# Two transformer layers on one Trainium2 core: the opening's order list, and norm sums of three head groups moved behind the first transposes and widened to 80 columns

## The chip, the cores and the metric

The kernel runs on one core of one Trainium2 chip. The time is device time of the whole program in microseconds (us); lower is better. Inside the core, TensorE (PE) multiplies matrices into the eight PSUM banks, ScalarE (ACT) does exponentials and other functions, VectorE (DVE) and GpSimd (POOL) do elementwise work, and SyncE (SP) issues the DMAs.

## What is computed

Two layers, each an attention block and a mixer block, over 2048 tokens of 448 features in bf16:

```python
def _A_ref(x, wqkv, wo):              # 16 heads of 28 features
    qkv = (x @ wqkv).reshape(B, S, 3, H, Dh) ...
    scores = einsum("bhqd,bhkd->bhqk", q, k) * (Dh ** -0.5)
    p = softmax(scores); o = einsum("bhqk,bhkd->bhqd", p, v)
    return o.reshape(B, S, D) @ wo

x = x + _A_ref(layernorm(x), A_wqkv, A_wo)
x = x + _B_ref(layernorm(x), B_w1, B_w2, B_w3, B_w4)   # token-shift mixer and a gelu MLP
...                                                    # and both once more, same weights
```

All inputs are drawn at random; x and the weights of the attention have a scale of 0.05.

## The kernel before

The 16 heads lie in four groups of four; a group's four heads take the four 32-row strips of TensorE. Tokens lie in 16 tiles of 128. Scores are computed transposed (keys on partitions), exponentiated by ScalarE in pieces of two or three PSUM banks (L1822, `PT`), or for some pieces by VectorE and GpSimd (L1703 to L1720), and multiplied with V (L1855). Instead of a row maximum the softmax uses a bound: it adds to Q's 29th row a shift made of the largest squared norm of K (`kmaxc`), and takes off a multiple of Q's own squared norm. The multiples come from the norms of the weight columns of Q and K.

Those norms are what the change touches. `wnorm(s)` in `t_setup` makes them, with s = 0 for head group 0 and s = 1 for groups 1 to 3. It squares the weights of K and Q (L1275 on ScalarE or L1277 on VectorE), adds each column over 448 rows with matmuls against a column of ones (L1282: 8 matmuls for s = 0, 24 for s = 1), copies the sums to `csum` (L1286), adds them per head with the 0/1 matrix `a28` (L1287), copies to `wsum` (L1289), and with a few small operations (L1291 to L1302, a power on GpSimd at L1296) makes `ACOL` and `RTN`. Q's update (L1511) needs the first, the bias (L1613) the second.

The opening, before the first exponential, holds: the loads of x and of the K, Q and V weights; layer-norm statistics of the first four tiles (L1345 to L1447), their normalized copies `xn` (L1449 or L1451), the transposes on TensorE (`pe_transpose`, L1403) and their copies to `xT` (L1409 or L1411); K and Q projections of the four groups (`kq_proj`: four column strips of 32 in each of four 512-column matmuls, L1458), whose PSUM results are evicted with a scale (L1463, L1465, L1470), squared (L1474 or L1478) and summed per head (L1195); V projections (L1195) and their evictions (L1531).

The order of work isn't that of the source. A planner runs all generators twice against a table of costs (`dur`, `lat`, `svc`) and makes a list of operations for each engine. `OTHER` then names operations that go to their second engine (`alt`: an eviction to ScalarE in place of VectorE, for instance, or the other way round), and `ENGINE_ORDER` permutes each engine's list; in its text the numbers are, in turn, how many entries to take and how far to jump. `follow` walks the permuted lists, assigns PSUM banks, derives the semaphore waits, and calls `keep_pe_busy`: where its costs leave a gap on TensorE that is long enough, and TensorE's use over the last 4 us of its reckoning is not above 80%, it puts in 256-column matmuls of ones into a free bank (filler, L2246), whose result nobody reads. `GATE1` to `GATE3` name events that some generators wait for in the planner.

Each engine runs its list strictly in order. In the plan of dependencies, `reads` and `writes` are keys such as `("wst", 1)` for K's weights; a key in `reads` makes an operation wait for whoever writes it.

Of the kernel before, what the change touches and what calls it, by code (L numbers as in the profile page):

```python
# [756 lines left out]
def build_kernel(nc, A_x, A_wqkv, A_wo, B_x, B_w1, B_w2, B_w3, B_w4, out, n_layers=2):  # L757
    S = A_x.shape[1]
    D = 448
# [343 lines left out]
    def c_act(n):  # L1103
        return 0.08 + n * 0.000833
# [1238 lines left out]
```

## Time and profile before

| | |
|---|---|
| median of 3 runs | 1023.48 us (1022.03 to 1023.53) |
| profiled execution | 1021.86 us, span 1020.1 us |
| mean granted TensorE clock | 0.998 |
| busy in the span | ACT 985.9, PE 960.7, DVE 830.3, POOL 164.0 us |

A span is the time from the first to the last instruction on record. A row of a group gives line, engine, operation, output and input by the program's names, the number of instructions, busy time, the mean duration in ns, and the idle time ahead of them with what ended it. A row of the timeline gives the start, the time to the end of the last of the merged instructions, and then the same names; instructions that run one into the other are merged, and matmul ends are modelled.

### The profile page before, as it was taken

How to read it: one execution, taken by the hardware profiler on the slowest of the kernel's cores; microseconds unless marked ns; L12 is line 12 of the kernel's file. 1: busy time of each engine (PE TensorE's matmuls, PEld its weight loads, DVE VectorE, ACT ScalarE, POOL GpSimd, SP SyncE). 2: the span in 40 equal slices, each digit the busy share in tenths (PEclk: the TensorE clock that was granted, in tenths of full speed). 3: DMA queues.
4: the chain of work that ended last, by engine and by line, in shares of the span. 5: the costliest groups of instructions: out<-in, count | busy, mean ns of one | idle time of the engine just before them, and what ended most of it. 6: DMA issues, size and time to landing. Idle time of an engine off the chain costs nothing.

```text
span 1020.1 us, 24089 instructions
## 1 busy us (share of the span) xinstructions
PE 960.7 (94%) x10399; PEld 362.4 (36%) x10414; DVE 830.3 (81%) x1868; ACT 985.9 (97%) x941; POOL 164.0 (16%) x187
## 2 busy tenths in 40 slices
PE   9989899999999999999999999988999999999998
PEld 5322222333232333332343443332233233444456
DVE  8987887788978779888788888788888878878663
ACT  6999999999999999999999999999999999999983
POOL 3000101201110112112122020012222020121211
PEclk9999999999999999999999999999999999999999
DMA  5245311010101002210111101411020000110000
GB/s 140 55 102 148 87 37 22 3 36 1 22 1 22 2 1 43 38 22 1 22 43 32 28 22 43 115 43 42 22 38 8 14 20 6 22 31 2 11 11 23
DMA packets 70722, 35.21 MB, mean 35 GB/s; under 512 B 56472, under 2 KB 65048, under 8 KB 70616
## 3 DMA queue, kind: packets, MB, share of 16 engines
q1 hardware_dynamic: 70616, 33.68, 14.3%
q8 instruction: 81, 1.33, 0.5%
q14 instruction: 25, 0.20, 0.1%
HBM read 12.70 MB, written 7.08 MB: 19 GB/s over the span
## 4 chain that ended last, share of the span: by engine, by line
ACT 83%; PE 13%; DMA 1%; DVE 1%; SPq 0%; issue 0%; DVEq 0%
ACT PT L1822 76%; PE ps L1192 4%; ACT h2T L2211 4%; PE ps L1794 3%; PE ps L1195 3%; PE ps L1855 2%; ACT gt L1992 1%; PE ps L1458 1%; ACT L2211 1%; DMA uin<-uscr 1%; DMA wk_raw<-in_A_wqkv_dram 1%; ACT L1822 0%; DMA uscr<-uin 0%; DVE uin L1900 0%; SPq L1397 0%
## 5 line engine op out<-in xcount | busy, mean ns | idle before, releaser
L1822 ACT ACTIVATE PT<-ps 128x1024 bf16<-128x1024 f32 (+1 forms) x821 | 886.4, 1252 | 5.4 <-PE ps L1794 3.7
L1794 PE MATMUL ps<-qT,kT 32*128 32x512 bf16 x1536 | 247.3, 384 | 38.8 <-ACT PT L1822 28.9
L1855 PE MATMUL ps<-PT,vaug 128*32 128x512 bf16 (+1 forms) x2181 | 268.1, 361 | 2.5 <-ACT PT L1822 0.8
L1794 PEld LDWEIGHTS ps<-qT,kT 32*128 32x128 bf16 x1536 | 61.4, 91 | 243.8 <-ACT PT L1822 190.5
L1716 POOL TENSOR_TENSOR gt<-gt 128x512 f16<-128x512 f16 x55 | 59.8, 1088 | 473.8 <-DVE gt L1714 470.7
L1855 PEld LDWEIGHTS ps<-PT,vaug 128*32 128x32 bf16 x2181 | 76.8, 94 | 106.5 <-issue 76.4
L1192 PE MATMUL ps<-xT,w 112*128 112x512 bf16 (+6 forms) x514 | 105.9, 320 | 0.1
L1703 DVE TENSOR_SCALAR t<-ps 128x512 int32<-128x512 f32 x112 | 76.6, 684 | 25.1 <-PE ps L1794 23.7
L2171 DVE CAST h2T<-ps 128x512 bf16<-128x512 f32 (+2 forms) x126 | 72.3, 581 | 26.3 <-PE ps L1192 13.2
L1794 PE MATMUL ps<-kT 32*128 32x256 bf16 (+1 forms) x768 | 82.8, 310 | 8.0 <-ACT PT L1822 5.4
L1720 DVE SCALAR_TENSOR_TENSOR PTD<-t,gt 128x512 uint16<-128x512 int32 x112 | 78.2, 701 | 5.4 <-PE ps L1855 1.9
L1195 PE MATMUL ps<-xT,w 112*32 112x512 bf16 (+3 forms) x1048 | 81.9, 344 | 0.6 <-DVE h2T L2171 0.6
L1717 DVE SCALAR_TENSOR_TENSOR gt<-gt,t 128x512 f16<-128x512 f16 x112 | 77.7, 695 | 4.7 <-POOL gt L1716 3.7
L2246 PE MATMUL ps<-ones_bf 128*128 128x256 bf16 x334 | 60.6, 282 | 1.8 <-DVE wk_raw L1246 1.2
L1195 PE MATMUL ps<-w,h2T 128*32 128x448 bf16 x932 | 57.7, 353 | 1.8 <-ACT h2T L2211 1.5
L1192 PEld LDWEIGHTS ps<-xT,w 112*128 112x128 bf16 (+1 forms) x514 | 40.9, 103 | 43.0 <-issue 23.4
L1192 PE MATMUL ps<-w,h2T 128*128 128x448 bf16 x215 | 52.1, 355 | 0.0
L1714 DVE TENSOR_SCALAR gt<-t 128x512 f16<-128x512 uint16 x112 | 48.5, 436 | 1.6
L1794 PEld LDWEIGHTS ps<-kT 32*128 32x128 bf16 x768 | 23.2, 91 | 74.8 <-ACT PT L1822 54.7
L2211 ACT ACTIVATE h2T<-h2T 128x7168 bf16<-128x7168 bf16 (+2 forms) x9 | 44.9, 5012 | 0.1
L1458 PE MATMUL ps<-xT,wq_raw 112*32 112x512 bf16 (+1 forms) x576 | 44.7, 363 | 0.3 <-issue 0.3
L1458 PE MATMUL ps<-xT,wk_raw 112*32 112x512 bf16 (+3 forms) x640 | 42.9, 348 | 0.4 <-DVE hT L1959 0.4
(157 smaller groups left out, 1148.6 us busy)
## 6 DMA issues: line engine op xcount, KB each, us to landing
uin<-uscr SPq DMA_DIRECT2D x20, 256.0 KB, 2.7
uscr<-u_sb SPq DMA_DIRECT2D x12, 256.0 KB, 2.1
uscr<-uin SPq DMA_DIRECT2D x8, 256.0 KB, 2.2
out_dram<-uin SPq DMA_DIRECT2D x16, 112.0 KB, 1.7
w<-in_B_w_dram SPq DMA_DIRECT2D x4, 392.0 KB, 5.1
x_res<-in_A_x_dram SPq DMA_DIRECT2D x3, 448.0 KB, 8.7
w<-in_B_w_dram SPq DMA_DIRECT2D x2, 448.0 KB, 4.0
w<-in_B_w_dram SPq DMA_DIRECT2D x4, 196.0 KB, 4.0
```

Source lines behind the costliest of these rows:

```text
L1192: return e.matmul(out=dst(0, m), lhsT=lhs(0, m), rhs=rhs() if callable(rhs) else rhs, start=start, stop=stop)
L1195: return [e.matmul(out=dst(a, min(m, a + 32)), lhsT=lhs(a, min(m, a + 32)), rhs=rhs() if callable(rhs) else rhs, start=start, stop=stop, t ...
L1458: yield op("pe", c_mm(nw) + Sched.COLT, lambda e, b=b, fc=fc, rows=rows: [e.matmul(out=ps[32 * j:32 * j + 32, bi(b), 0:nw], lhsT=w[0:rows, ...
L1703: yield op("dve", c_ps(512), lambda e: e.tensor_scalar(out=t32[:, ti.n, :], in0=ps[:, bk, :], scalar1=0.0, scalar2=65536.0, op0=ALU.max, o ...
L1717: yield op("dve", c_ps(512), lambda e: e.scalar_tensor_tensor(out=half(), in0=half(), scalar=EXPV * 2.0 ** -16, in1=frac(), op0=ALU.add, o ...
L1720: yield op("dve", c_ps(512), lambda e: e.scalar_tensor_tensor(out=PTD[:, to.n, :].bitcast(mybir.dt.uint16), in0=t32[:, ti.n, :], scalar=2. ...
L1794: yield op("pe", 0.005 if ph == h else 0.012 + W / 2400.0, lambda e, bk=bk, r0=32 * j, g=g, kc=kc, qt=qt, q0=q0, W=W, c0=W * h: e.matmul(o ...
L1822: yield op("act", e_dur(n), lambda e, b0=b0, p0=p0, cnt=cnt: e.activation(out=PT[:, p0:p0 + cnt, :], in_=ps[:, b0:b0 + cnt, :], func=ACT.E ...
L1855: return e.matmul(out=ps[32 * j:32 * j + 32, UBK, 0:128 * nt], lhsT=vaug[:, vs, 32 * (4 * g + j):32 * (4 * g + j) + 32], rhs=rhs(), start= ...
L2171: yield op("dve", c_ps(NW), lambda e, fch=fch, b=b: e.tensor_copy(out=h2T[:, fch, hoff:hoff + NW], in_=ps[:, bi(b), 0:NW]), reads=[("ps", ...
L2211: yield op("act", c_act(14 * NW), lambda e, c0=c0, NW=NW: e.activation(out=h2T[:, :, c0:c0 + NW], in_=h2T[:, :, c0:c0 + NW], func=ACT.Gelu ...
L2246: SC.fill = (0.13, lambda e, b: e.matmul(out=ps[:, bi(b), 0:256], lhsT=ones_bf[:, :], rhs=ones_bf[:, :].unsqueeze(1).to_broadcast([128, 2, ...
```

## The change

Four things are edited. First, the 24 sums of `wnorm(1)` also read `("lnT", k)` for k = 0 to 3, a new key that the copy of a transposed tile (L1409 or L1411) writes; for `wnorm(0)` that list is empty. `GATE3`, which was empty, makes the planner start `wnorm(1)` after the event `("ln", 0, 0)`, when the first four tiles have been transposed. Second, every sum of both `wnorm` is taken against 80 columns of ones in place of one, into 80 PSUM columns, of which the copy to `csum` reads the first; the second product goes to column 480 in place of 16. Third, figures of the planner's cost table are changed: evictions and squares on ScalarE in the opening are 0.1 to 0.27 us longer, and loads of weights and x have other latencies. These emit nothing by themselves. Fourth, `ENGINE_ORDER` and `OTHER` are new throughout: for all five engines, from the first entries to the last. The ScalarE list covers 928 operations (927 before), VectorE's 1861 (1868), GpSimd's 189 (183), TensorE's 6702 and SP's 110 as before, the filler not counted. `OTHER` has 135 entries, 132 before.

```diff
-            "0 2 1 3 1 -3 1 2 1 -7 1 -2 1 4 1 2 2 19 2 -28 1 27 8 -20 1 -2 1 -9 ...
+            "0 1 1 -2 1 5 1 -3 1 2 1 -6 1 13 1 -3 2 -3 1 -2 1 4 2 -9 1 -8 1 4 2 ...
...
-    GATE3 = None
+    GATE3 = ('ln', 0, 0)
...
-   ld_w(ci): ... dma=True, dma_time=(7.4, 6.4)[ci], lat=(2.8, 3.6)[ci], svc=1.7)
+   ld_w(ci): ... dma=True, dma_time=(7.4, 6.4)[ci], lat=(3.5, 3.6)[ci], svc=1.7)
...
-                    yield op("act", c_act(4 * nc), lambda e, i=i, w=w: e.activation(out=wsqs[i]...
+                    yield op("act", 0.1 + c_act(4 * nc), lambda e, i=i, w=w: e.activation(out=wsqs[i]...
...
-                                out=ps[0:112, bi(b), ng * i + k:ng * i + k + 1], lhsT=wsqs[i]..., rhs=ones_bf[0:112, 0:1],
+                                out=ps[0:112, bi(b), 80 * (ng * i + k):80 * (ng * i + k) + 80], lhsT=wsqs[i]..., rhs=ones_bf[0:112, 0:80],
                                 start=(fc == 0), stop=(fc == 3)),
-                                reads=[keys[i], ("ones_bf",)], writes=[("ps", bi(b))], touch=[b])
+                                reads=[keys[i], ("ones_bf",)] + [("lnT", k) for k in range(4 * s)], writes=[("ps", bi(b))], touch=[b])
-   tensor_copy(out=csum[0:112, o:o + 2 * ng], in_=ps[0:112, bi(b), 0:2 * ng])
+   tensor_copy(out=csum[0:112, o:o + 2 * ng], in_=ps[0:112, bi(b), 0:160 * ng].rearrange("p (c r) -> p c r", r=80)[:, :, 0])
-   matmul(out=ps[:, bi(b), 16:16 + 2 * ng], lhsT=a28[:, :], ...), and the copy from it to wsum
+   matmul(out=ps[:, bi(b), 480:480 + 2 * ng], lhsT=a28[:, :], ...), and the copy from it to wsum
...
-        def pe_transpose(xs, xt, i):
+        def pe_transpose(xs, xt, i, also=()):
...
-                     reads=[("ps", bi(b))], writes=[xt.part(i)], touch=[b],
+                     reads=[("ps", bi(b))], writes=[xt.part(i)] + list(also), touch=[b],
...
-            yield op("act", c_act(D), lambda e: e.activation(out=blk(xs.v[:, i, :]), ...
+            yield op("act", 0.27 + c_act(D), lambda e: e.activation(out=blk(xs.v[:, i, :]), ...
...
-            yield from pe_transpose(xs, xt, i)
+            yield from pe_transpose(xs, xt, i, [("lnT", i)])
...                                     # in kq_proj, the ScalarE alternatives:
-   alt("act", c_act(nw), ...)           +   alt("act", 0.16 + c_act(nw), ...)    # eviction
-   alt("act", c_act(nw), ...)           +   alt("act", 0.18 + c_act(nw), ...)    # with a bias
-   alt("act", c_act(nw), ...)           +   alt("act", 0.1 + c_act(nw), ...)     # square
```

More of the change, by code (lines that the diff above doesn't have):

```diff
@@ L1228, in ld_w @@
                 return op("sp", 0.1, lambda e: e.dma_start(out=raw[ci][:, :, 0:D], in_=A_wqkv[:, ci * D:(ci + 1) * D].rearrange("(c p) n -> p c n", p=112)),
-                          writes=[(("wst", ci), "w")], dma=True, dma_time=(7.4, 6.4)[ci], lat=(2.8, 3.6)[ci], svc=1.7)
+                          writes=[(("wst", ci), "w")], dma=True, dma_time=(7.4, 6.4)[ci], lat=(3.5, 3.6)[ci], svc=1.7)
             for h in range(2):
                 yield op("sp", 0.1, lambda e, h=h: e.dma_start(out=x_res[:, 2 * h:2 * h + 2, :], in_=xin[:, 2 * h:2 * h + 2, :]),
-                         writes=[("x", 2 * h), ("x", 2 * h + 1)], dma=True, dma_time=3.0 + 0.5 * h, lat=1.9, svc=(0.7, 1.9)[h])
+                         writes=[("x", 2 * h), ("x", 2 * h + 1)], dma=True, dma_time=3.0 + 0.5 * h, lat=1.9, svc=0.7)
             yield ld_w(1)
@@ L1274, in wnorm @@
                     w = raw[1 - i]
-                    yield op("act", c_act(4 * nc), lambda e, i=i, w=w: e.activation(out=wsqs[i][0:112, :, lo:lo + nc], in_=w[:, :, lo:lo + nc], func=ACT.Square),
+                    yield op("act", 0.1 + c_act(4 * nc), lambda e, i=i, w=w: e.activation(out=wsqs[i][0:112, :, lo:lo + nc], in_=w[:, :, lo:lo + nc], func=ACT.Square),
                              reads=[("wst", 1 - i)], writes=[keys[i]],
@@ L1282, in wnorm @@
                             yield op("pe", 0.06, lambda e, fc=fc, i=i, k=k, g=g, b=b: e.matmul(
-                                out=ps[0:112, bi(b), ng * i + k:ng * i + k + 1], lhsT=wsqs[i][0:112, fc, 112 * g:112 * g + 112], rhs=ones_bf[0:112, 0:1],
+                                out=ps[0:112, bi(b), 80 * (ng * i + k):80 * (ng * i + k) + 80], lhsT=wsqs[i][0:112, fc, 112 * g:112 * g + 112], rhs=ones_bf[0:112, 0:80],
                                 start=(fc == 0), stop=(fc == 3)),
-                                reads=[keys[i], ("ones_bf",)], writes=[("ps", bi(b))], touch=[b])
-                yield op("dve", 0.1, lambda e, b=b: e.tensor_copy(out=csum[0:112, o:o + 2 * ng], in_=ps[0:112, bi(b), 0:2 * ng]), reads=[("ps", bi(b))], writes=[("csum", s), ("wsqread", s)], touch=[b])
-                yield op("pe", 0.06, lambda e, b=b: e.matmul(out=ps[:, bi(b), 16:16 + 2 * ng], lhsT=a28[:, :], rhs=csum[0:112, o:o + 2 * ng], start=True, stop=True),
+                                reads=[keys[i], ("ones_bf",)] + [("lnT", k) for k in range(4 * s)], writes=[("ps", bi(b))], touch=[b])
+                yield op("dve", 0.1, lambda e, b=b: e.tensor_copy(out=csum[0:112, o:o + 2 * ng], in_=ps[0:112, bi(b), 0:160 * ng].rearrange("p (c r) -> p c r", r=80)[:, :, 0]), reads=[("ps", bi(b))], writes=[("csum", s), ("wsqread", s)], touch=[b])
+                yield op("pe", 0.06, lambda e, b=b: e.matmul(out=ps[:, bi(b), 480:480 + 2 * ng], lhsT=a28[:, :], rhs=csum[0:112, o:o + 2 * ng], start=True, stop=True),
                          reads=[("csum", s), ("a28",)], writes=[(("ps", bi(b)), "h")], touch=[b])
-                yield op("dve", 0.1, lambda e, b=b: e.tensor_copy(out=wsum[:, o:o + 2 * ng], in_=ps[:, bi(b), 16:16 + 2 * ng]), reads=[("ps", bi(b))], writes=[("wsum", s)], touch=[b])
+                yield op("dve", 0.1, lambda e, b=b: e.tensor_copy(out=wsum[:, o:o + 2 * ng], in_=ps[:, bi(b), 480:480 + 2 * ng]), reads=[("ps", bi(b))], writes=[("wsum", s)], touch=[b])
                 yield ("rel", b)
@@ L1317, in t_setup2 @@
             yield op("sp", 0.1, lambda e: e.dma_start(out=wv[0:112, :, :], in_=A_wqkv[:, 2 * D:3 * D].rearrange("(c p) n -> p c n", p=112)),
-                     writes=[("wst", 2)], dma=True, dma_time=4.5, lat=2.8, svc=1.7)
+                     writes=[("wst", 2)], dma=True, dma_time=4.5, lat=3.5, svc=1.7)
             yield op("pool", 0.6, lambda e: e.memset(xn[:, :, :].rearrange("p i (c r) -> p i c r", r=128)[:, :, :, 112:128], 0.0), writes=[("xnpad",)])
@@ L1321, in t_setup2 @@
                 yield op("sp", 0.1, lambda e, c=c: e.dma_start(out=x_res[:, 4 * c:4 * c + 4, :], in_=xin[:, 4 * c:4 * c + 4, :]),
-                         writes=[("x", 4 * c + i) for i in range(4)], dma=True, dma_time=4.0 + 1.2 * (c - 1), lat=1.9, svc=1.2)
+                         writes=[("x", 4 * c + i) for i in range(4)], dma=True, dma_time=4.0 + 1.2 * (c - 1), lat=3.4, svc=1.4)
                 yield ("sig", ("xld", c))
@@ L1448, in first_tile @@
                      reads=[("mv", i), ("rstd", i)], writes=[("vpe", i)])
-            yield op("act", c_act(D), lambda e: e.activation(out=blk(xs.v[:, i, :]), in_=b112(x_res[:, i, :]), func=ACT.Identity, scale=rstd[:, i:i + 1], bias=vpe[:, i:i + 1]),
+            yield op("act", 0.27 + c_act(D), lambda e: e.activation(out=blk(xs.v[:, i, :]), in_=b112(x_res[:, i, :]), func=ACT.Identity, scale=rstd[:, i:i + 1], bias=vpe[:, i:i + 1]),
                      reads=[("x", i), ("vpe", i), ("rstd", i)], writes=[xs.part(i)],
@@ L1464, in kq_proj @@
                          reads=[("ps", bi(b)), ("cols",)], writes=dkeys, touch=[b],
-                         alt=[alt("act", c_act(nw), lambda e, b=b: e.activation(out=dst, in_=ps[:, bi(b), 0:nw], func=ACT.Identity, scale=mul))])
+                         alt=[alt("act", 0.16 + c_act(nw), lambda e, b=b: e.activation(out=dst, in_=ps[:, bi(b), 0:nw], func=ACT.Identity, scale=mul))])
             else:
@@ L1469, in kq_proj @@
                     reads=[("ps", bi(b)), bkey, ("cols",)], writes=dkeys, touch=[b],
-                    alt=[alt("act", c_act(nw), lambda e, b=b: e.activation(out=dst, in_=ps[:, bi(b), 0:nw], func=ACT.Identity, scale=mul, bias=bias))])
+                    alt=[alt("act", 0.18 + c_act(nw), lambda e, b=b: e.activation(out=dst, in_=ps[:, bi(b), 0:nw], func=ACT.Identity, scale=mul, bias=bias))])
             yield ("rel", b)
@@ L1477, in kq_proj @@
                      reads=dkeys, writes=[("sq", si)],
-                     alt=[alt("act", c_act(nw), lambda e: e.activation(out=sq[:, si.n, 0:nw], in_=dst, func=ACT.Square))] if early else [], lk=1)
+                     alt=[alt("act", 0.1 + c_act(nw), lambda e: e.activation(out=sq[:, si.n, 0:nw], in_=dst, func=ACT.Square))] if early else [], lk=1)
             b2 = yield ("acq", MISC, [("sq", si)])
```

526 rows, old and new, of tables (ENGINE_ORDER, OTHER) are left out of this document.

## The prediction, before the changed kernel was run

> **What bounds the kernel now.** I read the page first, then busy time by stage, then who waited for whom, then the opening instruction by instruction.
>
> ```profile
> span 1020.1 us, 24089 instructions
> ...
> PE 960.7 (94%) x10399; PEld 362.4 (36%) x10414; DVE 830.3 (81%) x1868; ACT 985.9 (97%) x941; POOL 164.0 (16%) x187
> ```
> ```profile
> 0.00:22.20 22.20, 20.38 (x267) 12.74 (x268) 17.26 (x76) 14.13 (x21) 7.86 (x21) 0.92 0.55 139
> 22.20:100.00 77.80, 72.59 (x748) 23.63 (x751) 66.61 (x175) 77.67 (x75) 3.06 (x3) 1.00 0.43 106
> ```
> ```profile
> 22.22 5.98 ACT L1822 ACTIVATE PT<-ps 128x1536 bf16<-128x1536 f32 x5
> ```
>
> Columns of the stage rows: stretch, length, then busy time (and instructions) of PE, PEld, DVE, ACT and POOL, granted TensorE clock, DMA share, GB/s. ScalarE is busy 97% of the span (VectorE 81%). From its first exponential at 22.22 it works almost without a break (77.67 of 77.80 us in the next stretch). So the end is set by when that stream begins, by how much work ScalarE has, and by its few waits. Before 22.2 it works only 14.13 us: 22.20 - 14.13 = 8.07 us of the opening are idle. What it waited for, over the whole run and then between 22.2 and 985 us (total, times, longest):
>
> ```profile
> ACT kT L1470 <- PE ps L1458: 2.0, 1, 2.0
> ACT qT L1465 <- PE ps L1458: 1.4, 1, 1.4
> ```
> ```profile
> ACT PT L1822 <- PE ps L1794: 3.7, 10, 0.5
> ACT PT L1822 <- PE ps L1855: 0.7, 2, 0.4
> ACT gt L1992 <- DVE gw L1991: 0.3, 1, 0.3
> ```
>
> The middle of the run holds 3.7 + 0.7 + 0.3 = 4.7 us of waits, spread over thirteen places. The opening holds 2.0 + 1.4 = 3.4 us in two places, and both wait for the K and Q projections on TensorE (L1458). The other 4.7 us of the opening's idle time lie ahead of the first weights and are not touched by the change. Why TensorE is late there is in the granted clock, the third column from the right:
>
> ```profile
> 8.00:9.00 1.00, 0.46 (x11) 0.37 (x8) 0.43 (x2) 1.00 (x2) 0.19 (x1) 1.00 1.08 303
> 9.00:10.00 1.00, 1.00 (x22) 1.00 (x21) 0.89 (x2) 1.00 (x3) 0.00 (x0) 1.00 1.09 379
> 10.00:11.00 1.00, 1.00 (x23) 0.97 (x25) 1.00 (x3) 0.75 (x2) 0.00 (x0) 0.98 1.13 282
> 11.00:12.00 1.00, 1.00 (x12) 0.34 (x8) 0.30 (x3) 0.00 (x0) 0.00 (x0) 0.50 1.14 222
> 12.00:13.00 1.00, 1.00 (x16) 0.43 (x12) 0.93 (x2) 0.25 (x1) 0.00 (x0) 0.50 1.13 237
> 13.00:14.00 1.00, 1.00 (x16) 0.42 (x12) 1.00 (x3) 0.97 (x2) 0.00 (x0) 0.50 0.80 241
> 14.00:15.00 1.00, 1.00 (x20) 0.45 (x16) 1.00 (x6) 0.19 (x1) 0.00 (x0) 0.81 0.02 8
> 15.00:16.00 1.00, 1.00 (x22) 0.39 (x18) 0.15 (x3) 0.41 (x1) 0.00 (x0) 1.00 0.00 0
> ```
> ```profile
> 10.12 0.81 PE L1282 MATMUL ps<-ones_bf,w 112*112 112x1 bf16 x13
> 10.86 1.85 PE L1458 MATMUL ps<-xT,wk_raw 112*32 112x512 bf16 x16
> 19.08 1.03 PE L1458 MATMUL ps<-xT,wq_raw 112*32 112x512 bf16 x16
> ```
> ```profile
> 10.93 4.63 PE ps L1458 x52
> 15.57 0.02 issue
> 15.59 0.69 ACT qT L1465
> ```
>
> The clock falls to half just when the projections begin. Read from the rows, the stretch is 0.04 us before 11, three whole microseconds, and 0.38 us after 14: about 3.42 us. The same sixteen 512-column matmuls take 1.85 us inside it and 1.03 us later at full clock. The last fence is the chain of waits: 4.63 us of projections stand on it, then ScalarE. So this slow stretch lies on the path.
>
> **The change, part by part.** The norm sums (L1282) of groups 1 to 3, 24 one-column matmuls, ran between the transposes and the first projection, the last thirteen of all sums at 10.12. A PE that is busy with one-column matmuls (1.00 in the rows 9 to 11) still lost its clock, so it is not the busy time that keeps it. The change widens every sum to 80 columns, makes those 24 wait for all four transposed tiles, and so leaves waits on PE into which the scheduler puts its 256-column filler.
>
> First term, the clock. 3.42 us at half rate do the work of 1.71 us at full rate. If the filler and the wide sums hold the clock, the projections end 1.7 us earlier, and ScalarE's waits of 2.0 and 1.4 us shrink by that. Bounds: -1.7 and 0; I take -1.7. [...]
>
> Second term, the place of the sums.
>
> ```profile
> 9.89 0.75 DVE L1409 COPY xT<-ps 112x512 bf16<-112x512 bf16 x2
> ```
> The last transposed tile is in place at 9.89 + 0.75 = 10.64, and the first projection starts at 10.86: the sums in front cost about 0.2 us. They go behind it: -0.2 (bounds -0.2 and 0).
>
> Third term, the sums in their new place.
>
> ```profile
> 9.64 0.41 PE L1403 MATMUL ps<-ident,xn 128*112 128x128 bf16 x4
> ```
> The trace shows no 80-column matmul of this kind. The nearest below is the one-column sum, 0.81/13 = 0.062 us, the nearest above a 128-column transpose, 0.41/4 = 0.10 us. So 24 cost 1.5 to 2.4 us of TensorE. Both are bounded by the weight loads that they share, and 0.062 is nearer in kind; I take 1.5. They are hidden if they stand where TensorE runs ahead of ScalarE:
>
> ```profile
> L1470 ACT ACTIVATE kT<-ps,cols 128x512 bf16<-128x512 f32 x3 | 2.3, 773 | 2.0 <-PE ps L1458 2.0
> L1478 ACT ACTIVATE sq<-kT 128x512 bf16<-128x512 bf16 x3 | 1.9, 626 | 0.1
> ```
> An eviction with its square is 0.773 + 0.626 = 1.40 us of ScalarE against 1.03 us for its sixteen projection matmuls, so with VectorE's share of evictions the lead is thin at first. The order list of TensorE has a long unbroken run of entries after some fifteen others behind the transposes, which I read as these sums behind the first K and Q projections. I take 0, and keep +1.5 as the upper bound. Their results are late too, but with slack:
>
> ```profile
> 23.77 0.22 DVE L1298 TENSOR_SCALAR sc<-sc,cols 128x3 f32<-128x3 f32 x1
> ```
> The factor for groups 1 to 3 is used only from 23.77; queued behind the waiting sums on TensorE are further projections, and ScalarE's evictions wait for those.
>
> Fourth term, the new orders and the moves between engines. Counting the entries that each order list covers, ScalarE goes from 927 to 928 operations, VectorE from 1868 to 1861, GpSimd from 183 to 189. From the numbers in the list of moved operations, the layer-1 part has one more K eviction on ScalarE (128 columns) and the tail one copy fewer, so the opening has one more. One more eviction or square in the opening is +0.65 (0.626 to 0.773). The small one is 0.28 by the nearest shape below:
>
> ```profile
> L2053 ACT ACTIVATE hT<-ps 112x128 bf16<-112x128 f32 x8 | 1.7, 279 | 2.3 <-PE ps L1192 2.3
> ```
> It may use up a wait; +0.1. The copy saved in the tail counts nothing, since ScalarE waits for TensorE there. Against that, of the 3.4 us of waits 3.4 - 1.7 - 0.2 = 1.5 remain, and the opening's order is made with evictions priced 0.1 to 0.27 us higher, nearer the rows above. I take -0.9 of these 1.5 (bounds -1.5 and +0.5).
>
> Fifth term, the rest of the run. All order lists differ to the end, but ScalarE's list keeps the sequence of exponentials almost throughout. 4.7 us of waits can be lost at most; I take -0.3, bounds -1.5 and +4.5 (twelve more waits of 3.7/10 = 0.37 us).
>
> Edits with one answer: the changed latencies, durations and the gate in the source are the planner's figures and emit nothing; the wide PSUM regions (80 columns a sum, 480 for the six sums, the second product at column 480) stay within one bank of 512; the strided copy of the sums still reads six values. On the DMA queue the list starts with the same five entries, so the loads of x, K and Q keep their order.
>
> Sum: -1.7 - 0.2 + 0 + 0.65 + 0.1 - 0.9 - 0.3 = -2.35 us. The profiled execution took 1021.86 us, 1.8 us more than its span, and the median of the runs is 1023.48 (1022.03 to 1023.53). Against its own time the sum gives 1019.5; against the median, which is what is compared, 1021.1.
>
> **The rivals.** A: the clock falls all the same, and the sums now stand in the slow stretch. For it: PE was busy 1.00 from 9 to 11 and lost the clock, and the 16 transposes were part of that; filler needs gaps, and in the row 8 to 9 half a microsecond of PE was idle and got none. Against it: 42 filler matmuls of this width run from 1.2 us on, and the clock is full after them.
>
> ```profile
> 1.21 6.17 PE L2246 MATMUL ps<-ones_bf 128*128 128x256 bf16 x42 [1.21 <-DVE wk_raw L1246]
> ```
> The price: no -1.7, and 24 sums at 0.10 us (0.062 doubled, as the projections nearly double, is 0.12) are 2.4 us among projections that ScalarE waits for. -0.2 + 2.4 + 0.65 + 0.1 - 0.3 = +2.65, so 1026.1; it decides for slower once the sums cost more than 1.8 us there. [...] I give it 0.18: 0.13 slower, 0.05 within.
>
> B: the opening gains, and the new order of TensorE gives it back in the middle, by scores that come 0.37 us late a few times more. Six more such waits cost 2.2 us: 1021.1 + 2.2 = 1023.3, no change. Twelve would make it slower (1025.5). For it: every list is permuted to the end. Against: ScalarE was late by only 4.7 us in 960 under a like list. Chance 0.18: 0.10 within, 0.06 slower, 0.02 faster.
>
> C: the middle gains too, 1.5 instead of 0.3, and the opening's last 0.6 us of waits go: 1021.1 - 1.8 = 1019.3. Chance 0.12, all faster. That the wide sums do nothing and only the order counts is part of A.
>
> **How the numbers follow.** The forecast has 0.52. 0.2% of the median, about what a measurement of this kernel can tell from no change, is 2.05 us: faster means below 1021.43, slower above 1025.53. The forecast lies only 0.3 us inside; its own range, 1020.0 to 1022.6 (the third term at +1.5 at one end; the last 0.6 of the waits gained and the fifth term at -0.8 at the other), gives 0.36 faster and 0.16 within. Faster: 0.36 + 0.02 + 0.12 = 0.50; within: 0.16 + 0.05 + 0.10 = 0.31; slower: 0.13 + 0.06 = 0.19. The range 1018.6 to 1025.8 takes in C, B and about half of A.
>
> **What would show it.** Right: granted clock 1.00 from 10 to 15 us; filler matmuls between 8 and 10.7; the wait for L1458 ahead of the first K eviction about 1.1 us instead of 2.0; the first exponential near 20.5 instead of 22.2; waits of L1822 between there and the end near 4.4 us. Wrong: 0.50 in any of those rows, sums of L1282 on the chain of waits between projections, the first exponential no earlier than 22, or a total of L1822's waits above 7 us.

## The result and the profile after

The changed kernel takes 1029.13 us (median of 8 runs, 1027.57 to 1037.75) against 1021.51 us (8 runs, 1020.13 to 1023.53): a ratio of 1.0085, 95% interval 1.006 to 1.0109 (the medians alone give 1.0075; two of the runs took 1037.5 and 1037.8 us). It is some 0.8% slower. The forecast was 0.2% faster, and the time lies outside its range. The profiled execution took 1029.86 us, 8.0 us more than the one of before.

The page, then its stages (same columns as before):

```profile
span 1028.1 us, 23876 instructions
...
PE 965.7 (94%) x10293; PEld 363.6 (35%) x10310; DVE 834.3 (81%) x1861; ACT 989.9 (96%) x942; POOL 168.7 (16%) x193
```
```profile
0.00:22.20 22.20, 20.44 (x249) 12.60 (x250) 17.50 (x75) 15.07 (x21) 7.75 (x21) 1.00 0.58 139
...
11.00:12.00 1.00, 1.00 (x24) 0.54 (x20) 1.00 (x2) 0.66 (x1) 0.00 (x0) 1.00 1.15 231
12.00:13.00 1.00, 1.00 (x28) 0.48 (x20) 1.00 (x4) 0.62 (x1) 0.00 (x0) 1.00 1.13 209
13.00:14.00 1.00, 1.00 (x24) 0.39 (x16) 1.00 (x5) 0.96 (x3) 0.00 (x0) 1.00 0.88 214
```

The clock is held: 1.00 from 11 to 14, where it was 0.50. Even so the first exponential comes no earlier. The timeline of ScalarE:

```profile
12.38 0.78 ACT L1470 ACTIVATE kT<-ps,cols 128x512 bf16<-128x512 f32 x1 [0.72 <-PE ps L1458]
...
17.52 0.63 ACT L1478 ACTIVATE sq<-kT 128x512 bf16<-128x512 bf16 x1 [0.96 <-PE ps L1192]
...
22.55 1.45 ACT L1822 ACTIVATE PT<-ps 128x1536 bf16<-128x1536 f32 x1
```

22.55 against 22.22. The chain of waits says why: it now runs on TensorE from the first projection to the last V projection, with the norm sums in between.

```profile
10.02 0.40 PE ps L1282 x4
10.42 0.44 PE ps L2246 x4
10.86 3.35 PE ps L1458 x60
14.21 0.54 PE ps L1282 x8
14.74 0.00 PE ps L1287
14.75 0.09 PE ps L1282
14.83 0.33 PE ps L1458 x4
15.16 0.48 PE ps L1282 x7
...
16.35 0.54 PE ps L1282 x8
...
20.33 1.76 PE ps L1195 x36
22.09 0.02 issue
22.11 0.54 ACT vaug L1531
```

The sums behind 14 us (L1282) take 0.54 + 0.09 + 0.48 + 0.54 = 1.65 us of this chain. The rest of the loss lies behind the opening. Starts of exponentials (counted from 0) in the traces, and how much later than in the trace of before:

| exponential | before, us | after | later by |
|---|---|---|---|
| 0 | 22.2 | 22.6 | 0.34 |
| 20 | 46.2 | 47.0 | 0.83 |
| 100 | 132.3 | 133.6 | 1.29 |
| 120 | 153.4 | 155.8 | 2.43 |
| 320 | 386.1 | 389.1 | 3.05 |
| 500 | 606.3 | 612.3 | 6.02 |
| 740 | 884.0 | 891.1 | 7.10 |
| 820 (last) | 983.4 | 990.9 | 7.57 |

The loss comes in steps of 0.3 to 1.2 us; another 0.4 us lies behind the last exponential. ScalarE's waits between 22.5 and 992 us (total, times, longest) are twice those of before, which were 4.7 us:

```profile
ACT PT L1822 <- PE ps L1794: 8.0, 17, 0.7
ACT PT L1822 <- PE ps L1855: 1.0, 4, 0.4
```

From the start of the first exponential to the end of the last it takes 969.61 us instead of 962.32. Of these 7.29 us, 4.63 are idle time and 2.65 work: one more square (0.52 us not overlapped), one more K eviction (0.38), 1.85 us in the exponentials, and 0.1 less elsewhere. The 1.85 us belong to the waits as well. In both traces an exponential that follows on another instruction of ScalarE without a pause overlaps with its end, and adds 0.92 us (1024 columns) or 1.34 us (1536); one that starts behind a pause or a table load adds 1.02 or 1.45. So each interruption costs 0.107 us beside its own length. The trace of before has 36 such starts, this one 53, and 17 x 0.107 = 1.82 us. (Worked out from the starts and ends of all 821 exponentials.)

What a late score looks like, around exponential 357 and exponential 738:

```profile
431.90 0.67 DVE L1467 TENSOR_SCALAR kT<-ps,cols 128x384 bf16<-128x384 f32 x1
...
432.62 0.40 PE L1195 MATMUL ps<-sq,astat 128*32 128x512 bf16 x4 [0.59 <-DVE kT L1467]
...
433.39 0.60 PE L1794 MATMUL ps<-qT,kT 32*128 32x512 bf16 x5
...
433.82 1.02 ACT L1822 ACTIVATE PT<-ps 128x1024 bf16<-128x1024 f32 x1 [0.73 <-PE ps L1794]
...
886.73 0.61 PE L1195 MATMUL ps<-xT,w 112*32 112x512 bf16 x7 [0.80 <-DMA xT<-xn]
...
887.81 0.39 PE L1794 MATMUL ps<-kT 32*128 32x256 bf16 x6
...
888.25 1.45 ACT L1822 ACTIVATE PT<-ps 128x1536 bf16<-128x1536 f32 x1 [0.73 <-PE ps L1794]
```

In the first case the head of TensorE's list is a norm matmul (the sum of Q's squares per head) that waits 0.59 us for a K eviction on VectorE, which ends at 431.90 + 0.67 = 432.57 (why it waits for that eviction, the view doesn't say). In the second case a mixer matmul waits 0.80 us for a transposing DMA. The scores stand behind it in the list, and ScalarE loses 0.73 us each time.

One step is of another kind. From 141.6 to 145.0 us this execution ran at half clock:

```profile
138.40:141.80 3.40, 3.04 (x17) 0.85 (x14) 3.30 (x7) 3.40 (x4) 0.00 (x0) 0.97 0.01 2
141.80:145.20 3.40, 3.40 (x20) 0.59 (x18) 2.29 (x6) 2.54 (x3) 0.00 (x0) 0.53 0.02 5
```

ScalarE works 2.54 of 3.40 us there, and the delay grows from 1.29 to 2.43 us between exponentials 100 and 120.

### The profile page after: what moved, and what is told of

The parts are those of the page before. It is cut to its first block, busy times and chain, and to the rows that moved or that the text cites. A ratio compares the mean times of both kernels' runs of the same rounds, so it can differ in the third digit from the quotient of the medians.

```text
span 1028.1 us, 23876 instructions
## 1 busy us (share of the span) xinstructions
PE 965.7 (94%) x10293; PEld 363.6 (35%) x10310; DVE 834.3 (81%) x1861; ACT 989.9 (96%) x942; POOL 168.7 (16%) x193
## 4 chain that ended last, share of the span: by engine, by line
ACT 79%; PE 17%; DVE 2%; DMA 1%; issue 0%; SPq 0%; POOL 0%; DVEq 0%
ACT PT L1822 73%; PE ps L1192 5%; PE ps L1794 4%; ACT h2T L2211 4%; PE ps L1195 4%; PE ps L1855 2%; PE ps L1458 1%; ACT gt L1992 1%; ACT L2211 1%; DMA wq_raw<-in_A_wqkv_dram 1%; DMA xT<-xn 1%; ACT L1822 0%; PE ps L1403 0%; PE ps L1282 0%; PE ps L2246 0%
## 5 line engine op out<-in xcount | busy, mean ns | idle before, releaser
L1822 ACT ACTIVATE PT<-ps 128x1024 bf16<-128x1024 f32 (+1 forms) x821 | 887.7, 1247 | 10.3 <-PE ps L1794 8.0
L1794 PE MATMUL ps<-qT,kT 32*128 32x512 bf16 x1536 | 250.4, 385 | 38.2 <-ACT PT L1822 28.7
L1855 PE MATMUL ps<-PT,vaug 128*32 128x512 bf16 (+1 forms) x2181 | 264.8, 361 | 3.1 <-ACT PT L1822 1.6
L1716 POOL TENSOR_TENSOR gt<-gt 128x512 f16<-128x512 f16 x59 | 63.6, 1081 | 440.5 <-DVE gt L1714 415.7
L1855 PEld LDWEIGHTS ps<-PT,vaug 128*32 128x32 bf16 x2181 | 75.6, 95 | 106.3 <-issue 77.5
L1195 PE MATMUL ps<-xT,w 112*32 112x512 bf16 (+3 forms) x1060 | 86.2, 345 | 1.1 <-DMA xT<-xn 0.8
L1192 PE MATMUL ps<-w,h2T 128*128 128x448 bf16 x242 | 58.8, 354 | 0.7 <-ACT h2T L2211 0.7
L1195 PE MATMUL ps<-w,h2T 128*32 128x448 bf16 x824 | 52.4, 353 | 1.6 <-ACT h2T L2211 1.4
L1458 PE MATMUL ps<-xT,wq_raw 112*32 112x512 bf16 (+1 forms) x576 | 46.2, 359 | 0.2
```

Of the source, the lines that this page charges most:

```text
L1192: return e.matmul(out=dst(0, m), lhsT=lhs(0, m), rhs=rhs() if callable(rhs) else rhs, start=start, stop=stop)
L1195: return [e.matmul(out=dst(a, min(m, a + 32)), lhsT=lhs(a, min(m, a + 32)), rhs=rhs() if callable(rhs) else rhs, start=start, stop=stop, t ...
L1458: yield op("pe", c_mm(nw) + Sched.COLT, lambda e, b=b, fc=fc, rows=rows: [e.matmul(out=ps[32 * j:32 * j + 32, bi(b), 0:nw], lhsT=w[0:rows, ...
L1716: yield op("dve", c_f2b(512), lambda e: e.tensor_tensor(out=half(), in0=half(), in1=half(), op=ALU.mult), reads=[("gt", x)], writes=[("gt" ...
L1794: yield op("pe", 0.005 if ph == h else 0.012 + W / 2400.0, lambda e, bk=bk, r0=32 * j, g=g, kc=kc, qt=qt, q0=q0, W=W, c0=W * h: e.matmul(o ...
L1822: yield op("act", e_dur(n), lambda e, b0=b0, p0=p0, cnt=cnt: e.activation(out=PT[:, p0:p0 + cnt, :], in_=ps[:, b0:b0 + cnt, :], func=ACT.E ...
```

## The experiments

Where a kernel mixes two orders, every operation of one part keeps the relative order and the engine that it has in the one kernel, and every other operation those of the other; the filler follows by the same rule as always. Each text on what was expected stood before the run. Theory R is that the order lists behind the opening cost the time, rival O that the opening does.

**The changed kernel's opening, the rest of before.**

```diff
 ENGINE_ORDER, OTHER:
-    changed kernel's lists throughout
+    changed kernel's lists to 44 us of the planner's time, behind that those of the kernel before
```

> The changed kernel's source with its own order up to 44 us of the planner's time (439 operations) and the order and engine choice of the kernel before for all that follows. Theory R (the loss sits in the new order lists behind the opening): about 1022, some 0.3 to 0.9 us above the kernel before, first exponential near 22.5, ScalarE's waits for scores back near 4.4 us. Rival O (the opening sets everything back, by late K, Q or V): about 1028 to 1029.

1023.39 us (11 runs), ratio 1.002 (1.001 to 1.003), somewhat above what R gave (1022). The first exponential starts at 22.72, the last is 1.59 us late against the trace of before. Its waits (here the helper lines are three numbers lower):

```profile
ACT PT L1819 <- PE ps L1791: 4.1, 11, 0.5
ACT PT L1819 <- PE ps L1852: 1.2, 2, 0.8
```

**The opening of before, the changed kernel's rest.**

```diff
 ENGINE_ORDER, OTHER, with the source of before:
-    lists of before throughout
+    lists of before to 44 us of the planner's time, behind that the changed kernel's
```

> The mirror image: the source and the opening order (468 operations, to 44 us) of the kernel before, and behind that the changed kernel's order and engine choice. Theory R: 1028 to 1029, ScalarE waiting 9 to 10 us for scores behind the first exponential. Rival O: about 1022.

1029.94 us (6 runs), ratio 1.0081 (1.006 to 1.0102), somewhat above what R gave (1028 to 1029): nearly the whole loss without the edits of the opening. Its waits (lines one number higher) hold a half-clock stretch of 10.24 us from 140.35:

```profile
ACT PT L1823 <- PE ps L1795: 9.4, 19, 1.2
ACT PT L1823 <- PE ps L1856: 1.6, 5, 0.6
```

So R holds for the larger part and O falls as the main cause: the opening of the changed kernel costs 0.2%, the lists behind it 0.8%. The two sum to more than the changed kernel loses. Runs whose mean granted clock is 1.00 leave the clock out of the comparison, and give the same order:

| kernel, runs at a mean clock of 1.00 | runs | median, us |
|---|---|---|
| before | 23 | 1020.23 |
| changed opening, rest of before | 9 | 1023.23 |
| opening of before, changed rest | 2 | 1027.62 |
| changed | 3 | 1027.64 |

The clock is thus not what makes the changed kernel slower: 7.4 us are lost without a half-clock stretch.

**Only the middle.**

```diff
 ENGINE_ORDER, OTHER, with the source of before:
-    lists of before throughout
+    changed kernel's lists for the 2080 operations between exponentials 330 and 505
```

> The kernel before, with the changed kernel's order and engine choice only between exponentials 330 and 505 (2080 operations, where layer 0 ends and layer 1 begins); before and behind that, the order of before. Between these the changed kernel lost 3.0 us against before in the traces (from +3.0 to +6.0). If the loss is local and additive: +2.5 to +3.5 us in that stretch, none outside it, about 1024.5. If an order only loses because of the state that it starts from: less than 1 us.

1025.08 us (5 runs), ratio 1.0038 (1.0024 to 1.0052). Against the trace of before, its exponential 320 is 0.95 us early, exponential 560 is 2.47 late, and from there to the end nothing is added or given back. The stretch costs 3.4 us and stays local, as expected. ScalarE's waits for scores from 400 to 615 us, in the kernel before and then in this one:

```profile
ACT PT L1822 <- PE ps L1794: 1.0, 3, 0.5
```
```profile
ACT PT L1822 <- PE ps L1794: 4.0, 8, 0.8
```

Five new waits make 3.0 us, and the extra K eviction 0.38.

The 0.95 us at exponential 320 come from the opening. It is that of the kernel before in every operation, with one-column sums and no filler between them, and yet this execution kept its clock there; the transposes started at 7.94 instead of 7.26:

```profile
7.94 0.55 PE L1403 MATMUL ps<-ident,xn 128*112 128x128 bf16 x7
...
10.77 1.05 PE L1458 MATMUL ps<-xT,wk_raw 112*32 112x512 bf16 x16
```

The first sixteen projection matmuls take 1.05 us, not 1.85, and the first exponential starts at 20.85. The mixed kernel with the opening of before kept its clock there too, and starts it at 20.99. So the 22.22 of the trace of before is that of an opening which lost its clock. Against one that kept it the changed opening is 1.6 to 1.7 us late, not 0.34.

**Late scores moved ahead of what blocked them.**

```diff
 ENGINE_ORDER["pe"] of the changed kernel, for exponentials 91, 357, 434, 498 and 738:
-    blocked operations, then scores
+    scores, then blocked operations
```

> The changed kernel with five groups of score matmuls moved forward in TensorE's order, each ahead of what it stood behind when its exponential came late (exponentials 91, 357, 434, 498 and 738, counted from 0; the waits ahead of them were 0.20, 0.73, 0.61, 0.46 and 0.73 us, 2.7 us together). If a blocked matmul at the head of TensorE's queue is all that makes these exponentials late: the five waits go and the last exponential starts 2 to 2.7 us earlier (about 1026 to 1027). Rival: TensorE and VectorE have no slack there, and the moved-back work makes a later score late by as much: the five waits go, others appear within ten exponentials, and the time is within 0.5 us of the changed kernel, or above it.

1029.33 us (median of three runs, 1028.92 to 1029.66; a fourth took 2740.89 us and is left out), ratio 1.0074 (1.0058 to 1.0089): no gain, as the rival said. All three have a mean clock of 1.00, and lie 1.7 us above the runs of the changed kernel that have it too. Four of the five waits are gone; the one at 91, which both traces put down to a product with V (L1855), is still there with 0.24 us. Others came within five exponentials: 0.34 at 361, 0.26 and 0.58 at 435 and 436, 0.16 at 500 and 501, 0.10 at 739 and, where a step of the mixer's gelu is now late, this one:

```profile
890.38 0.63 ACT L1992 ACTIVATE gt<-gw 112x512 f32<-112x512 f16 x1 [0.84 <-DVE gw L1991]
```

**Wide sums alone.**

```diff
-   out=ps[..., ng * i + k:ng * i + k + 1], rhs=ones_bf[0:112, 0:1]
+   out=ps[..., 80 * (ng * i + k):80 * (ng * i + k) + 80], rhs=ones_bf[0:112, 0:80]
```

in the kernel before, with the copies from the new columns and nothing else.

> The kernel before with one edit: all norm sums are 80 columns wide (same places, same order, no filler added). If the width alone keeps TensorE's clock: granted clock 1.00 from 11 to 14 us, first K eviction about 0.9 us earlier, 1.0 to 1.9 us faster in all (about 1020). If the transposes or the short pause at 8.2 us lose the clock: 0.50 as before, and 1021.5 to 1022.

> The kernel before with wide sums once more, to narrow its interval (0.9991, 0.9982 to 1.0001 so far). If the clock kept at the projections is worth what the first exponential shows (1.0 to 1.4 us): ratio 0.9986 to 0.9992, interval below 1. If the gain is only there in runs in which the kernel before loses its clock, and it keeps it in a third of them: the same ratio, with the kernel before spread over 1019.6 to 1023.8 and this one over 1020.1 to 1021.5 but for a few.

Ratios 0.9991 (0.9982 to 1.0001) and 0.9996 (0.9986 to 1.0007). The clock is 1.00 in both traces from 10 to 14 us, and in the second of them ScalarE's first eviction and first exponential come 0.64 and 1.54 us earlier than before:

```profile
11.00:12.00 1.00, 1.00 (x22) 0.56 (x24) 0.52 (x4) 0.00 (x0) 0.00 (x0) 1.00 1.14 231
```
```profile
12.11 0.78 ACT L1470 ACTIVATE kT<-ps,cols 128x512 bf16<-128x512 f32 x1 [1.26 <-PE ps L1458]
...
20.68 5.97 ACT L1822 ACTIVATE PT<-ps 128x1536 bf16<-128x1536 f32 x5
```

The measured gain is smaller, and the kernel before does not lose its clock in every run. Of its 56 runs beside the experiments, 23 report a mean clock of 1.00 and have a median of 1020.23 us, 21 report 0.998 (1021.73), 6 report 0.997 (1022.56), one 0.996 (1024.01) and 5 report 0.995 (1023.78). One stretch of 3.41 us at half clock makes 0.998 of a span of 1020 us, so one such stretch costs about 1.5 us, and the kernel before has one or more in 33 of 56 runs; in which of them it lies in the opening isn't known. With wide sums it is 16 of 23 runs at 1.00, median 1020.67; medians over all are 1020.70 against 1021.40. Among runs at 1.00, wide sums are thus 0.44 us slower than the kernel before: what they may gain comes from the clock alone. This is the only version that may beat both kernels, and neither interval excludes no change.

**Narrow sums in the changed kernel.** The reverse of the diff above.

> The changed kernel with its norm sums one column wide again; order, waits and filler unchanged. If the filler alone keeps the clock: 1.00 from 11 to 14 us and the time of the changed kernel within 0.3 us (1029). If the width is needed: 0.50 for some 3.4 us near 11 us and 1 to 1.7 us slower (1030 to 1031).

1027.84 us (6 runs), ratio 1.0064 (1.005 to 1.0077), clock 1.00 in the opening:

```profile
11.00:12.00 1.00, 1.00 (x24) 0.54 (x20) 1.00 (x4) 0.47 (x1) 0.00 (x0) 1.00 1.12 241
12.00:13.00 1.00, 1.00 (x28) 0.47 (x20) 1.00 (x4) 0.80 (x2) 0.00 (x0) 1.00 1.07 253
```

In this trace of the new order the clock is held with the filler and one-column sums. The first exponential starts at 22.28, 0.28 us earlier than with wide sums; three traces with the changed opening unaltered (the changed kernel, the first mixed kernel and scores first) start it between 22.55 and 22.88, so this is no more than their own spread. The median is 1.3 us below that of the changed kernel, where 0.3 was expected, but among runs at a mean clock of 1.00 the two are equal: 1027.72 (5 runs) and 1027.64 (3). So the width is worth nothing here. Its order behind the opening is the changed one, without a half-clock stretch in the profiled execution: its stream of exponentials takes 967.74 us, 5.4 more than before. Of the other 1.9 us of the changed kernel's 7.29, 1.1 are the stretch at 141 us (the table's step between exponentials 100 and 120); the rest was not taken apart.

**Fewer sums.**

```diff
-                        for fc in range(4):
+                        for fc in range(4 if s == 0 else 1):
```

in the first mixed kernel.

> The changed kernel's opening with the order of before behind it, and of the 24 sums of groups 1 to 3 only six are made (the first of each four; the other 18 are left out, so Q's correction and the bias of groups 1 to 3 are computed from a quarter of the sum). If the sums stand on TensorE's path to the first exponential: 18 x 0.06 to 0.07 us less, first exponential 0.9 to 1.3 us earlier than in the kernel with all sums (22.7). If they lie beside it: 22.5 to 22.7.

One execution, 1022.67 us. Timeline of ScalarE, lines two numbers lower:

```profile
21.64 1.45 ACT L1820 ACTIVATE PT<-ps 128x1536 bf16<-128x1536 f32 x1
...
29.52 1.02 ACT L1820 ACTIVATE PT<-ps 128x1024 bf16<-128x1024 f32 x1 [0.81 <-PE ps L1792]
```

22.72 - 21.64 = 1.08 us for 18 sums, 0.06 each, from one trace on each side (0.9 to 1.2 us against the three starts from 22.55 to 22.88): they stood on the path to the first exponential, as expected if they do. But the sixth exponential waits 0.81 us for scores, and exponential 20 is 0.99 us late against before, as it is with all sums. An earlier first exponential isn't yet a gain.

**More filler.**

```diff
-    TARGET = 0.8
+    TARGET = 0.95
```

in the changed kernel and in the kernel before with wide sums.

> The changed kernel with one figure changed: filler is allowed up to 95% use of TensorE in the planner's last 4 us instead of 80% (some 60 more filler matmuls; the order is the same). If the half-clock stretch near 141 us comes from too little work on TensorE there: granted clock 1.00 in every run, times within 1027.4 to 1028.4, none above 1029. If it comes from something else: as many runs at 0.99 to 0.998 as before (5 of 8). If more filler delays scores: slower by 0.5 us or more.

> The kernel before with wide sums and filler allowed up to 95% use (some 40 more filler matmuls, same order). If the remaining half-clock stretches (runs at 0.995 to 0.998) come from too little work on TensorE and filler costs nothing: clock 1.00 in every run, 1020.0 to 1020.8, ratio 0.998 to 0.999. If more filler delays scores, as 0.4 us of the opening in the changed kernel with more filler suggests: 1021 to 1022.

In the changed kernel (380 filler matmuls in the trace, 345 before the edit): 1028.53 us, ratio 1.0065 (1.0052 to 1.0077), clock 1.00 in all five runs; but between 124.8 and 141.8 us its trace has 13 filler matmuls against 12, so the filler there isn't shown to be the reason. At a mean clock of 1.00 it is 0.9 us slower than the changed kernel (1027.64). Its first exponential comes at 23.01, 0.1 us behind the latest of the three starts above. In the kernel before with wide sums (362 filler matmuls instead of 334): 1022.9 us, ratio 1.0019 (1.0009 to 1.0028), slower, with 5 of 12 runs still below 1.00. Filler isn't free: the first expectation for that kernel was wrong, and the loss is larger than the second allowed (1021 to 1022).

## Why the prediction was wrong

**First term, the clock: right in kind, not in what it is worth.** The clock is held (1.00 from 11 to 14 us), and the projections end earlier: 60 of them take 3.35 us of the chain, where 52 took 4.63. Where the opening of before kept its clock, the first exponential came 1.2 to 1.4 us earlier, not 1.7; and 23 of 56 runs of before have a mean clock of 1.00 anyway, so that over many runs only a part of this is to be had. The stretches found here lasted 3.41 us (at 11 in the trace of before, at 141 in that of the changed kernel), 6.83 (wide sums with more filler, from 707.84) and 10.24 (the opening of before with the changed rest, from 140.35): one, two and three times 3.41. Some runs of one and the same kernel had such a stretch and others had none; the term should have been weighed by a chance of that, and I took it whole.

**Second term:** the first projection starts at 10.79 instead of 10.86, not 0.2 us earlier, because the last sums of group 0 and four filler matmuls now stand ahead of it on the chain. There was also less to gain than I read: the last of the transposed tiles was not VectorE's, at 10.64, but ScalarE's, at 9.68 + 1.06 = 10.74:

```profile
9.68 1.06 ACT L1411 ACTIVATE xT<-ps 112x512 bf16<-112x512 bf16 x2
```

**Third term: taken at 0, near its upper bound of 1.5 in fact.** The sums stand between projections on the chain of waits, with 1.65 us; leaving out 18 of them gained 1.08 us, which makes about 1.4 for the 24. That cancels the first term. The sign that I needed was in the order list, a run of sums ahead of the later projections, with ScalarE's lead over TensorE only 0.4 us per projection in my own sum.

**Fourth term:** +0.65 came as 0.52 (a square, behind the first exponential), +0.1 as 0.38 (the K eviction is larger than the shape that I took), and the -0.9 of an order with better prices didn't come: the first exponential is 0.34 us late and exponential 20 is 0.83.

**Fifth term: this is the step that failed.** I took -0.3 with an upper bound of +4.5; the stream of exponentials became 7.3 us longer. Of that the two additional operations of the fourth term are 0.9, waits 4.6, and the interruptions that come with them 1.8. With its clock held (narrow sums) the stream is still 5.4 us longer, 4.5 without the two operations: all of my upper bound. What failed is the thought that a list which keeps ScalarE's sequence almost throughout also keeps its waits. ScalarE's sequence says nothing of when TensorE's and VectorE's work stands ahead of a score. I also priced a wait at its length alone. Rival B named the mechanism, "scores that come 0.37 us late a few times more", and I priced it at 2.2 us and gave slower a chance of 0.06 by it. The mixed kernel shows it alone: 0.8% with the opening of before, and 7.4 us at a mean clock of 1.00.

**The signs.** The granted clock, the filler ahead of the projections and the first wait (0.72 us) were as named for right. Three of the four signs for wrong came: sums on the chain between projections, the first exponential behind 22 us, and 9.0 us of waits of L1822 where 7 was the limit.

**Rival A** fell: the clock did not fall in the opening. Its price for the sums among the projections, 2.4 us, was nearer to the truth than my 0.

**What stays open.** Why the half-clock stretch near 141 us comes in some runs of the new order and not in others is not settled: narrow sums, which leave that stage untouched, had it in at most one of six runs. Two runs of the changed kernel, at 1037.5 and 1037.8 us with a mean clock of 0.988 and 0.990, were not profiled. What stood ahead of a late score was traced for two waits only, and moving scores forward did not recover the time; which entries of the lists cost it is open.

## What to carry to other kernels

An edit at one place that comes with a newly searched order list is two changes, and the list is the larger one: splice old and new lists at a point in time and measure each half before arguing about the edit. With the bound engine 96% busy, moving late scores forward in the list gained nothing here: five were moved, four of their waits went, other late operations appeared within five exponentials, and the time was 1029.33 us against 1029.13. A wait of that engine cost 0.107 us beside its length here, since its exponentials otherwise overlap with what is ahead of them (0.92 us added for 1024 columns, 1.02 behind a pause). A loss of clock that some runs have and others don't must be weighed by how many runs have it, not read from one profile; and two traces should have the same clock before a difference between them is put down to the edit.

## What the runs showed of the hardware that was not expected

In the trace of before TensorE ran only transposes and one-column sums from the end of the filler at 7.38 us to the first projection at 10.86, 3.48 us, and the clock then fell to half for 3.41 us. The same instructions kept the clock in the two traces in which that stretch was shorter, 2.67 and 2.44 us (only the middle; opening of before). With 80 columns it was kept in both traces, over a stretch of 3.57 and 3.58 us, and in the changed order, with eight filler matmuls between 7.4 and 10.9 us, with sums of either width. One lost clock is too few to say that the width decides.

The width of a sum cost next to nothing: thirteen sums take 0.81 us with one column and 0.84 with 80. The weight loads of the thirteen one-column sums (L1282, from 10.09 in the trace of before) take 0.75 us. The mean granted clock of a run, 1.00, 0.998, 0.997 or 0.995, sorts the medians of one kernel's runs: 1.5, 2.3 and 3.6 us above the first.
